# A planner that orders a fused attention and gated product: two projections in flight, a different choice of banks, choices redrawn every 8 phases, and separate buffers in the tail

## The chip, the cores and the metric

The kernel runs on one core of a Trainium2 chip. Times are microseconds of that core. The time before is 669.75 us, the median of three runs (669.70 to 669.76). In the tables TensorE is PE (its weight loads are PEld), ScalarE is ACT, VectorE is DVE, GpSimd is POOL, and SyncE, which issues most transfers, is SP.

## The reference

The inputs are bfloat16, 2048 rows of 512 elements. With `xn` the layer-normalised input, the output is `x + s * g`:

```python
xn = _layernorm(x)                                   # 2048 x 512
q  = (xn @ wq) in 32 heads of 16;  k = xn @ wk;  v = xn @ wv   # one k and one v for all heads
p  = softmax(q k^T / sqrt(16))                       # 32 heads x 2048 x 2048
s  = (p v, heads side by side) @ wo                  # 2048 x 512
g  = silu(silu(xn @ w1) @ w2)                        # 512 -> 1792 -> 512
return x + s * g
```

The exponentials of 32 x 2048 x 2048 scores are most of the work.

## The kernel before

**No order is written by hand.** Python code in the kernel simulates the five engines with fixed durations (the class `Planner`) while the program is being made, and the order in which it places operations is the order of each engine's program. On the chip every engine runs its list in order, with semaphore waits. So the planner's choices are fixed in the program; nothing is decided at run time.

**The score tiles.** The scores are cut into 2048 tiles of 128 keys x 512 queries of one head. A tile's matmul uses only 32 rows of the TensorE array, so up to four tiles of different row groups run side by side. One such bundle is called a phase (`do_S`, L1001 on). Each tile fills one of seven PSUM banks (0 to 6); the eighth, `OB`, collects the attention output. A bank comes free when its exponential has been taken, in one of two ways:

- An A tile: ScalarE's Exp (L1717), for up to three banks in one instruction if they are equally spaced neighbours. The result goes to `pa_sb`, which has 26 slots; the number of slots in use is `a_pressure()`.
- A D tile: VectorE turns the score into the bit pattern of an approximate power (L1002) in `db_sb`. Three more shifted copies of it are made by GpSimd (L1202) in `ds_sb`, four tiles at a time.

**The products after it.** An A tile takes part in one matmul with V (L1282), a D tile in four. These matmuls have 32 columns, and four of different column groups run side by side; such a bundle of four is called a round here. Rounds of the attention product (`do_pv`) and rounds of the projections (L511) have the same shape. A change between a phase (32 rows x 128 columns) and rounds (128 x 32) is a change of the array's mode; the planner counts `SWITCH` 105 ns for it.

**The projections.** A job is one projection tile: 56 of kind `h` (w1, 4 rounds each), 16 `z` (w2, 14 rounds), 15 `q` (4 rounds) and 12 `w` (wo, 4 rounds) besides those of the start and the tail. A job takes a bank of the seven when it starts (`start_jobs`), runs its rounds between phases, and gives the bank back when the instruction that evacuates it has been placed: for `h` and `z` a tanh on ScalarE (L669) and then a product on VectorE (L671). Jobs start in the order of their pace (a share of the tiles assigned). `can_start` allows one such job at a time (two in the prologue), counted until the bank comes back, and none while `a_pressure()` is above `START_Z` 4 or `START_H` 8. Since a phase holds at most four tiles and leaves rows idle when it holds three, a `z` job can also run a quarter of one of its rounds in a phase's idle row group; these are called pieces (L618).

**A step of TensorE.** `pe_step` looks whether a phase is possible (`s_phase_ready`: at least three banks free, and not later than ScalarE needs it; a fourth bank is waited for only up to `STOL4` 0 ns past that), and otherwise places a round: of the attention if `a_pressure()` has reached a limit, else of a job, else of the attention. `do_S` decides how many tiles of the phase are D tiles: with four banks free `N4` 2 (`J4` 2 while a job is active), with three `N3` or `J3` 1, less if VectorE's backlog is long. Limits pass through `vary`, which multiplies them with a random factor within `SPREAD`. The random numbers come from a list of ten seeds, each used for `STRETCH` 64 phases.

**The tail.** The last four output tiles (r = 0 to 3) have no further scores beside them. Their product with wo ends in banks; r = 0 and 2 (`EVR`) are evacuated by ScalarE into `xn_sb` (L714) and multiplied by VectorE (L716), r = 1 and 3 are evacuated and multiplied by VectorE at once (L719). For r < 3 the result and the residual `xr_sb` are summed by TensorE with an identity matrix (L1503) and copied to `ob_sb` by ScalarE (L1508); for r = 3 VectorE adds (L731). The results lie in `fin_sb`, whose two halves alternate. The four stores are issued by SP (L725).

Of the kernel before, what the change touches and what calls it, by code (L numbers as in the profile page):

```python
# [46 lines left out]
MM = 216.0  # L47
BLG = 0
NEAR, AHEAD = 18, 0.6
SWITCH, SKEW = 105.0, 10.0  # L50
# [245 lines left out]
def bass_recurrent_scan__grouped_kv_mqa__dense_activation_silu__prompt_kernel(  # L296
# [30 lines left out]
    with ExitStack() as es:  # L327
# [56 lines left out]
        def vary(x):  # L384
            return x * (1.0 + SPREAD * (rng[-1].random() - 0.5)) if rng else x
        outs = []
        PH.clear()
# [112 lines left out]
        def job(kind, arg, pace, rounds, consume, preds=(), bk=None, mode="C", gate=None):  # L500
            jb = Job()
            jb.kind, jb.arg, jb.pace, jb.rounds, jb.consume = kind, arg, pace, rounds, consume
            jb.preds, jb.bank, jb.fixed, jb.mode, jb.gate = preds, bk, bk is not None, mode, gate
            jb.due, jb.pos, jb.end, jb.got, jb.left, jb.piece, jb.prev = None, 0, len(rounds), set(), len(rounds), None, None
            jb.tasks = {}
            jobs.append(jb)
            return jb
# [187 lines left out]
        def mk_z(tt, pace):  # L695
            c, r = divmod(tt, 4)

            def consume(jb, op):
# [10 lines left out]
                    lambda k, rows: w2_sb[rows, k, :], lambda k: ["w2", ("u", k)])  # L709

        def scaled(tt, b, r=None):
            k = tt % 2
            if r in EVR:
                ev = pl.add(Task(AC, 490.0, lambda a: a.activation(xn_sb[:, r, :], bank(b), ACT.Copy, scale=0.25),  # L714
                                 [("ps", b)], [("xn", r)], 0))
                fin_task[tt] = Task(DV, 333.0, lambda v: v.tensor_tensor(fin_sb[:, k, :], xn_sb[:, r, :], tmp_sb[:, tt % 8, :], ALU.mult),  # L716
                                    [("xn", r), ("tmp", tt % 8)], [("fin", k)], SC_PRIO, [ev, tmp_task[tt], fin_task.get(tt - 2)], ports=2)
                return fin_task[tt]
            fin_task[tt] = Task(DV, T_P, lambda v: v.scalar_tensor_tensor(  # L719
                out=fin_sb[:, k, :], in0=bank(b), scalar=0.25, in1=tmp_sb[:, tt % 8, :], op0=ALU.mult, op1=ALU.mult),  # L720
                [("ps", b), ("tmp", tt % 8)], [("fin", k)], 0 if r is None else SC_PRIO, [tmp_task[tt], fin_task.get(tt - 2)])
            return fin_task[tt]
# [4 lines left out]

        def final(tt, b):
            k = tt % 2
            t1 = scaled(tt, b)  # L730
            t2 = Task(DV, 333.0, lambda v: v.tensor_tensor(ob_sb[:, tt % 4, :], fin_sb[:, k, :], xr_sb[:, tt % 4, :], ALU.add),  # L731
                      [("fin", k), ("xr", tt % 4)], [("ob", tt % 4)], -1, [t1, xr_task[tt], out_task.get(tt - 4)], ports=2)
            fin_task[tt], out_task[tt] = t2, store(tt, t2)
            return t1, t2
# [54 lines left out]
        for tt in range(NT - 4):  # L789
            specs.append((2 * NOC * (tt // 4 + 1) + 1.2 + 0.5 * (tt % 4), 2, ("w", tt)))  # L790
        specs.sort()
        for pace, _, sp in specs:
# [140 lines left out]
        def s_phase_ready():  # L933
# [20 lines left out]
            n = min(n, 4)  # L954
            while n > NMIN and bt[n - 1][0] > need + STOL4:
                n -= 1
# [3 lines left out]
            if n < 4:  # L960
                r = max(r, need - EARLY)
            return r
# [43 lines left out]
        def do_S(t):  # L1006
# [8 lines left out]
            if n <= 1:  # L1015
                want = 1 if ab > 2 * a_low else 0
            elif n == 2:
                want = 1 if ab > a_low else 0
            else:
                queue = sum(len(q) for g in range(st["gO"], min(st["gO"] + 2, NG)) for q in pvq[g])  # L1020
                held = any(not a.fixed for a in active)
                if held:
                    want = J4 + (queue < vary(Q4)) if n == 4 else J3 + (queue < vary(Q3))
                else:
                    want = N4 if n == 4 else max(N3, 2 * (queue < vary(QUEUE)))
                if ab > a_low:
                    want = 2
            pj = None
            late = [b for r, b in bank_times()[n:] if r <= t + LATE]
            if bl > one or not want_d():  # L1030
# [28 lines left out]
            banks = sorted(banks[:len(sl) + nd])  # L1059
            best = None  # L1060
            for c in combos(banks, len(sl)):
                key = (len(c) > 1 and len(set(y - x for x, y in zip(c, c[1:]))) > 1, c[-1] - c[0])
                if best is None or key < best[0]:
                    best = (key, c)
            abanks = best[1]
            solo = False
            if SOLO and len(sl) == 3:
# [70 lines left out]
            if dslots:  # L1138
                make_shifts()
            return True  # L1140

# [185 lines left out]
        def make_norm(g):  # L1327
# [6 lines left out]
            if g == NG - 1:  # L1334
# [9 lines left out]
                rcp_sb[:, k, :].unsqueeze(2).to_broadcast([P, NQ // 32, DH]), ALU.mult),  # L1344
                [("F", k), ("rcp", k)], [("otr", oi % 2, e)], -1, [t2, t2_task.get(oi - 2)], ports=2))
            norm[("m", g)] = t3
# [27 lines left out]
        def can_start(jb, pro):  # L1374
            near = not pro and closing()
            if jb.pace > progress() + (AHEAD if near else 1e-9):
# [5 lines left out]
            if not pro and not near and a_pressure() > (START_Z if jb.kind == "z" else START_H):  # L1382
# [48 lines left out]
        def finish(jb, op):  # L1431
            if jb.left == 0:
                tasks = jb.consume(jb, op)
                last = tasks[-1]

                def fin(op, jb=jb):
# [16 lines left out]
        def make_tail():  # L1453
# [20 lines left out]
        def tail_round(t):  # L1474
# [11 lines left out]
            for n, (r, part) in enumerate(tail["sums"]):  # L1486
# [3 lines left out]
                if part == 0 and (xr_task.get(tt) is None or xr_task[tt].op is None or len(tail["items"]) > 3):  # L1490
                    continue
                rr = pl.ready(PE, [("fin", tt % 2)] if part else [("xr", tt % 4)], () if part else [("ps", tb[4 + r])]) if tb[4 + r] in pool_free else INF
                if rr <= t + 20:
# [4 lines left out]
        def do_tail(t, it):  # L1498
            if it[0] == "s":
                r, part = tail["sums"].pop(it[1])  # L1500
                tt = 4 * (NC - 1) + r
                src = fin_sb[:, tt % 2, :] if part else xr_sb[:, tt % 4, :]
                pl.place(PE, MM, lambda pe: pe.matmul(bank(tb[4 + r]), lhsT=ident[:, :], rhs=src, start=part == 0, stop=part == 1),  # L1503
                         [("fin", tt % 2) if part else ("xr", tt % 4)] + [("id", i) for i in range(4)], [("ps", tb[4 + r])],
                         t0=max(t, pe_start(pl.clk[PE], "F")))
# [54 lines left out]
        def pe_step():  # L1560
# [11 lines left out]
            lim = vary(PRESS if jr[0] != "go" else PRESS_Z if jr[1].kind == "z" else PRESS_H)  # L1572
            if pr and pr[0] == "go" and (a_pressure() >= lim or closing()):
                col = ("pv", pr[1])
# [106 lines left out]
        def act_step():  # L1681
# [10 lines left out]
            if q:  # L1692
                q = [u for u in q if u.vis <= max(t, q[0].vis) + 25]
                while len(q) > 1 and (len(set(y.bank - x.bank for x, y in zip(q, q[1:]))) > 1 or abs(q[1].bank - q[0].bank) != 1):
                    q.pop()
                if q[0].solo:
                    q = q[:1]
                elif len(q) > 1 and any(u.solo for u in q):
                    q = q[:[u.solo for u in q].index(True)]
                n = len(q)  # L1700
                while n:
# [118 lines left out]
```

## Time and profile before

| what | value |
|---|---|
| median of three runs | 669.75 us (669.70 to 669.76) |
| span of the profiled execution, first to last instruction | 667.9 us |
| PE, ACT, DVE, POOL busy | 657.8, 652.8, 613.6, 561.9 us |
| TensorE clock granted | 1.000 |
| score tiles: taken by ScalarE, by VectorE | 1312, 736 |
| matmuls (all kinds) | 8972 |

The page gives the profiled execution's span, and no other time of its own; the median of the runs stands 1.85 us above that span. A row of the list of groups reads: line, engine, operation, output and inputs, shape, number; then busy time in us and mean ns of one; then the engine's idle time before it and what ended it. Busy times are unions, and instructions of ScalarE, VectorE and TensorE overlap their neighbours, so the mean of one instruction is longer than the distance from its start to the next one's start. Where the text below counts phases, rounds or distances, they are counted over the trace's rows in order of time.

### The profile page before, as it was taken

Reading aid. Unit: us, or ns where it says so; the run is one execution under the profiler, and the core shown is the slowest. Engines: PE = TensorE matmul, PEld = TensorE weight load, DVE = VectorE, ACT = ScalarE, POOL = GpSimd, SP = SyncE. Lnnn points to the kernel's source line nnn. Section 1 sums busy time; section 2 is a strip of 40 time slices with the busy share of each in tenths; the row PEclk is TensorE's granted clock in tenths of the full one; section 3 lists DMA queues with packets and bytes.
Section 4 is the critical chain, followed back from the end, with each engine's and each line's share of the span. In section 5 each row is a group of like instructions: output and inputs, shape, how many; then the busy total and the mean of one; then the engine's idle time right before and its main releaser. Section 6 shows DMA issues by size and latency. Waiting matters only on the chain.

```text
span 667.9 us, 21230 instructions
## 1 busy us (share of the span) xinstructions
PE 657.8 (98%) x8972; PEld 190.3 (28%) x8973; DVE 613.6 (92%) x1093; ACT 652.8 (98%) x767; POOL 561.9 (84%) x560
## 2 busy tenths in 40 slices
PE   8999999999999999999999999999999999999997
PEld 4322222222222222222222222222222322222222
DVE  8989999999899999989999899999999999998995
ACT  6999999999999999999999999999999999999997
POOL 3059889999898889998989888999899989897972
PEclk9999999999999999999999999999999999999999
DMA  9500000000000000000000010000000000000000
GB/s 302 164 9 2 3 1 2 2 3 2 1 2 18 19 18 18 1 2 2 2 2 2 18 32 18 2 2 2 2 2 2 2 18 18 17 18 2 2 2 33
DMA packets 11501, 12.86 MB, mean 19 GB/s; under 512 B 1808, under 2 KB 10768, under 8 KB 11408
## 3 DMA queue, kind: packets, MB, share of 16 engines
q1 hardware_dynamic: 10928, 10.78, 5.0%
q8 instruction: 72, 1.18, 0.7%
q0 software_dynamic: 192, 0.46, 0.2%
q10 hardware_dynamic: 288, 0.26, 0.1%
q14 instruction: 21, 0.17, 0.1%
HBM read 8.95 MB, written 2.10 MB: 17 GB/s over the span
## 4 chain that ended last, share of the span: by engine, by line
PE 88%; ACT 6%; DVE 4%; issue 1%; DMA 0%; ACTq 0%; DVEq 0%
PE ps L1282 38%; PE ps L866 29%; PE ps L511 20%; ACT pa_sb L1717 6%; DVE db_sb L1002 1%; DVE stats_sb L458 1%; ACT t_sb L669 1%; DMA ds_sb<-in_A_x_dram 0%; DVE fin_sb L719 0%; PE ps L527 0%; DVE xnT_sb L538 0%; DVE xn_sb L487 0%; DVE ob_sb L731 0%; DVE mv_sb L462 0%; DVE on_sb L1316 0%
## 5 line engine op out<-in xcount | busy, mean ns | idle before, releaser
L1717 ACT ACTIVATE pa_sb<-ps 128x1024 bf16<-128x1024 f32 (+2 forms) x670 | 617.0, 1027 | 4.8 <-PE ps L866 3.5
L1202 POOL INT64_ADD ds_sb<-db_sb x544 | 554.0, 1040 | 64.2 <-DVE otr_sb L1342 31.7
L1002 DVE TENSOR_SCALAR db_sb<-ps 128x512 uint16<-128x512 f32 x736 | 475.4, 683 | 40.0 <-PE ps L866 28.6
L1282 PE MATMUL ps<-ds_sb,v_sb 128*32 128x512 bf16 x2208 | 268.7, 383 | 0.0
L866 PE MATMUL ps<-qt_sb,kt_sb 32*128 32x512 bf16 x2048 | 251.2, 384 | 3.9 <-ACT pa_sb L1717 0.9
L1282 PE MATMUL ps<-pa_sb,v_sb 128*32 128x512 bf16 x1316 | 240.9, 382 | 0.0
L1282 PE MATMUL ps<-db_sb,v_sb 128*32 128x512 bf16 x736 | 169.3, 383 | 0.0
L866 PEld LDWEIGHTS ps<-qt_sb,kt_sb 32*128 32x128 bf16 x2048 | 62.8, 91 | 276.7 <-ACT pa_sb L1717 151.2
L1282 PEld LDWEIGHTS ps<-ds_sb,v_sb 128*32 128x32 bf16 x2208 | 65.6, 95 | 62.3 <-issue 44.6
L511 PE MATMUL ps<-xnT_sb,w_sb 128*32 128x512 bf16 x896 | 71.7, 383 | 0.0
L1282 PEld LDWEIGHTS ps<-pa_sb,v_sb 128*32 128x32 bf16 x1316 | 58.8, 95 | 37.9 <-issue 24.7
L511 PE MATMUL ps<-w_sb,u_sb 128*32 128x512 bf16 x820 | 64.1, 383 | 0.0
L1282 PEld LDWEIGHTS ps<-db_sb,v_sb 128*32 128x32 bf16 x736 | 42.2, 95 | 20.2 <-issue 14.7
L669 ACT ACTIVATE t_sb<-ps 128x512 bf16<-128x512 f32 x72 | 44.9, 623 | 0.0
L671 DVE SCALAR_TENSOR_TENSOR u_sb<-t_sb,ps 128x512 bf16<-128x512 bf16 x56 | 38.2, 683 | 1.0
L618 PE MATMUL ps<-w_sb,u_sb 32*128 32x512 bf16 x76 | 29.2, 384 | 0.0
L511 PEld LDWEIGHTS ps<-xnT_sb,w_sb 128*32 128x32 bf16 x896 | 17.1, 94 | 26.1 <-issue 21.1
L1359 POOL DMA_DIRECT2D kt_sb<-kt_sb x4 | 2.3, 566 | 23.9 <-DVE var_sb L481 8.1
L1338 DVE STREAM_TRANSPOSE f_sb<-ps 128x512 f32<-128x512 f32 x31 | 21.9, 706 | 0.0
L511 PEld LDWEIGHTS ps<-w_sb,u_sb 128*32 128x32 bf16 x820 | 15.2, 95 | 22.5 <-issue 19.3
L511 PE MATMUL ps<-wo_sb,on_sb 128*32 128x512 bf16 x256 | 18.9, 383 | 0.0
L511 PE MATMUL ps<-xnT_sb,wq_sb 128*32 128x512 bf16 x240 | 18.7, 384 | 0.1
(74 smaller groups left out, 180.8 us busy)
## 6 DMA issues: line engine op xcount, KB each, us to landing
w_sb<-in_B_w_dram SPq DMA_DIRECT2D x2, 1792.0 KB, 13.4
xr_sb<-in_A_x_dram SPq DMA_DIRECT2D x16, 128.0 KB, 2.6
out_dram<-ob_sb SPq DMA_DIRECT2D x16, 128.0 KB, 1.7
ds_sb<-in_A_x_dram SPq DMA_DIRECT2D x3, 512.0 KB, 6.6
wq_sb<-in_A_wq_dram SPq DMA_DIRECT2D x1, 512.0 KB, 4.9
wo_sb<-in_A_wo_dram SPq DMA_DIRECT2D x1, 512.0 KB, 16.2
kt_sb<-kt_sb POOLq DMA_DIRECT2D x4, 112.0 KB, 3.7
ds_sb<-in_A_x_dram ACTq DMA_DIRECT2D x2, 128.0 KB, 2.9
```

The costliest lines, as they stand in the source:

```text
L458: ts_ = pl.add(Task(DV, 593.0, lambda v, t=t: v.bn_stats(stats_sb[:, t, :], x_tile(t)), [xkey(t)], [("st", t)], 1 + j, gate=(lambda j=j: S ...
L511: last = h.matmul(bank(b)[32 * j:32 * (j + 1), 0:n], lhsT=lhs(j), rhs=rhs, start=start, stop=stop, tile_position=(0, 32 * j), skip_group_c ...
L618: return (lambda pe: pe.matmul(bank(b), lhsT=lhs(k, rows, 0, P), rhs=rhs(k, rows), start=False, stop=last, tile_position=(32 * i, 0), skip ...
L669: t1 = Task(AC, 490.0, lambda a: a.activation(t_sb[:, k, :], src, ACT.Tanh, scale=scale), [held], [("t", k)], 0, [t0])
L671: t2 = Task(DV, T_P, lambda v: v.scalar_tensor_tensor(out=dst, in0=t_sb[:, k, :], scalar=1.0, in1=src, op0=ALU.add, op1=ALU.mult), [held, ...
L866: return pe.matmul(bank(b), lhsT=kt_sb[32 * i:32 * i + 32, g % 2, kt * P:(kt + 1) * P], rhs=qt_sb[32 * i:32 * i + 32, (g // 2) % NQR, :], ...
L1002: bt.P[i] = pl.add(Task(DV, T_P, lambda v: v.tensor_scalar(db_sb[:, bt.b, i * NQ:(i + 1) * NQ], bank(b), 128.0 * LOG2E, 128.0 * (SHIFT_BET ...
L1202: whole["po"].append(pl.add(Task(PO, T_P64, lambda g, cols=cols: g.int64_add(ds_sb[:, s, cols].bitcast(U64), db_sb[:, bt.b, cols].bitcast( ...
L1282: h = pe.matmul(bank(OB)[32 * i:32 * (i + 1), cols], lhsT=lhs, rhs=rhs, start=s0, stop=s1, tile_position=(0, 32 * i), skip_group_check=True)
L1338: t1 = pl.add(Task(DV, T_TR, lambda v: v.transpose(f_sb[:, k, :], bank(OB)), [("ps", OB)], [("F", k)], 1, [norm.get(("m", g - 2))]))
L1359: kt1[c] = pl.add(Task(PO, T_SWDGE, lambda e: e.dma_start(kt_sb[DH:P, 1, cols], kt_sb[0:P - DH, 0, cols]), [("kt0", k) for k in range(4 * ...
L1717: op = pl.place(AC, 0.8333 * NQ * n + T_AF, lambda a: a.activation(pa_sb[:, s * NQ:(s + n) * NQ].rearrange("p (b n) -> p b n", n=NQ), ps3[ ...
```

## The change

- `TWO = 1`: `can_start` counts only jobs that still have rounds to run against the limit, so a second job may start while the first one's bank waits for its evacuation. In all no more than two jobs outside the prologue hold a bank.
- `JPICK = 1`, `JTOL`: a starting job no longer takes the bank that comes free first, but among those free within 30 ns of it the one that leaves most neighbouring pairs among the other banks.
- `START_H` goes from 8 to 11.
- The seeds are 84 instead of 10, `STRETCH` is 8 instead of 64, `SPREAD` 0.4 instead of 0.3. After each phase `redraw` sets further choices at random: with a chance of 3% the number of D tiles of the next phase, with 3% that ScalarE's instruction takes one bank instead of a pair, with 10% whether a round of the attention or of a job goes first, with 10% that a D tile may join a phase up to 200 ns late, with 5% that a phase may wait up to 250 ns for a fourth bank, with 5% that a phase of fewer banks may start up to 400 ns sooner, and with 20% each which banks the A tiles and a starting job take.
- Tail: r = 0 and 2 use the halves of `fin_sb`, r = 1 and 3 their own tile of `xn_sb`; `EVR` is (1, 3), and only r = 0 and 1 (`SUMS = 2`) are summed by TensorE; r = 2 and 3 are added by VectorE.
- `CHAIN`, `BUNCH`, `APICK`, `PR_OTR`, `PR_OB` and `FAR` are new names whose values leave the code as it was.

```diff
-SEEDS, STRETCH, SPREAD = (4812, 312, 1660, 4615, 1697, 8414, 4190, 8770, 5102, 5729), 64, 0.3
+SEEDS = (
+    3820, 2220, 5745, 350, 5151, 6989, 5911, 6177, 6265, 4479, 5498, 6172, 361, 2787, 4955, 618,
...
+STRETCH, SPREAD = 8, 0.4
...
+TWO = 1
+JPICK, JTOL, APICK = 1, 30.0, 0
+R_WANT, R_SPLIT, R_FIRST, R_LATE, R_TOL, R_BANK = 0.03, 0.03, 0.1, 0.1, 0.05, 0.2
...
-START_Z, START_H = 4, 8
+START_Z, START_H = 4, 11
...
-RH, EVR, SC_PRIO, MT_EARLY = 6, (0, 2), 0, 1
+RH, EVR, SC_PRIO, MT_EARLY = 6, (1, 3), 0, 1
...
+        def redraw():
+            if not rng:
+                return
+            r = rng[-1]
+            pick.update(want=r.choice((0, 1, 2)) if r.random() < R_WANT else None, split=r.random() < R_SPLIT,
+                        first=r.choice(("pv", "job")) if r.random() < R_FIRST else None,
+                        late=r.random() * 200.0 if r.random() < R_LATE else 0.0,
+                        tol=r.random() * 250.0 if r.random() < R_TOL else 0.0,
+                        early=r.random() * 400.0 if r.random() < R_TOL else 0.0,
+                        abank=r.random() if r.random() < R_BANK else None, jbank=r.random() if r.random() < R_BANK else None)
...
+        def fin_of(tt, r=None):
+            if r is None or r % 2 == 0:
+                k = tt % 2 if r is None else r // 2
+                return fin_sb[:, k, :], ("fin", k)
+            return xn_sb[:, r, :], ("xn", r)
...
-            while n > NMIN and bt[n - 1][0] > need + STOL4:
+            while n > NMIN and bt[n - 1][0] > need + pick["tol"]:
...
+            if pick["want"] is not None:
+                want = min(pick["want"], n - 1)
...
-                if len([a for a in active if not a.fixed]) >= lim or not pool_free:
+                if len([a for a in active if not a.fixed and (a.left or not TWO)]) >= lim or not pool_free:
+                    return False
+                if TWO and not pro and len([a for a in active if not a.fixed]) >= 2:
                     return False
...
-                    jb.bank = min((r, b) for r, b in bank_times())[1]
+                    bt = bank_times()
+                    if JPICK:
+                        ok = [b for r, b in bt if r <= max(t, bt[0][0]) + JTOL]
+                        gone = [u.bank for u in units[st["expn"]:]]
+                        jb.bank = min(ok, key=lambda b: bank_key(b, pro_free(b), ok))
...
-            tail["sums"] = [(r, part) for part in range(2) for r in range(3)]
+            tail["sums"] = [(r, part) for part in range(2) for r in range(SUMS)]
...
-                if r < 3:
+                if r < SUMS:
                     stt[r] = pl.add(scaled(tt, tb[r], r))
                 else:
-                    for tk in final(tt, tb[r]):
+                    for tk in final(tt, tb[r], r):
                         pl.add(tk)
```

More of the change, by code (lines that the diff above doesn't have):

```diff
@@ L48 @@
 BLG = 0
+TWO = 1
+BUNCH = 0
+SUMS = 2
+FAR = 1
+JPICK, JTOL, APICK = 1, 30.0, 0
+PR_OTR, PR_OB = -1, -1
+CHAIN, AHEAD_T, START_T = '', 0.3, 11
+R_WANT, R_SPLIT, R_FIRST, R_LATE, R_TOL, R_BANK = 0.03, 0.03, 0.1, 0.1, 0.05, 0.2
 NEAR, AHEAD = 18, 0.6
@@ L385, in vary @@
             return x * (1.0 + SPREAD * (rng[-1].random() - 0.5)) if rng else x
+        pick = dict(want=None, split=False, first=None, late=0.0, tol=0.0, early=0.0, abank=None, jbank=None)
+        def redraw():
[8 more added lines that the diff above has]
+                        abank=r.random() if r.random() < R_BANK else None, jbank=r.random() if r.random() < R_BANK else None)
         outs = []
@@ L726, in store, with final @@
                                [("ob", tt % 4)], [("out", tt)], 0, [t2], dma=128 * 1024, on_place=outs.append))
[L728 to L732, printed above, removed]
+        def final(tt, b, r=None):
+            t1 = scaled(tt, b, r)
+            src, key = fin_of(tt, r)
+            t2 = Task(DV, 333.0, lambda v: v.tensor_tensor(ob_sb[:, tt % 4, :], src, xr_sb[:, tt % 4, :], ALU.add),
+                      [key, ("xr", tt % 4)], [("ob", tt % 4)], PR_OB if r is None else 1,
+                      [t1, xr_task[tt], out_task.get(tt - 4)], ports=2)
             fin_task[tt], out_task[tt] = t2, store(tt, t2)
@@ L791, in bass_recurrent_scan__grouped_kv_mqa__dense_activation_silu__prompt_kernel @@
         specs.sort()
+        if BUNCH:
+            specs = [(BUNCH * int(p / BUNCH) if sp[0] != "q" else p, k, sp) for p, k, sp in specs]
         for pace, _, sp in specs:
@@ L1027, in do_S @@
                     want = 2
+            if pick["want"] is not None:
+                want = min(pick["want"], n - 1)
             pj = None
-            late = [b for r, b in bank_times()[n:] if r <= t + LATE]
+            late = [b for r, b in bank_times()[n:] if r <= t + pick["late"]]
             if bl > one or not want_d():
@@ L1059, in do_S @@
             banks = sorted(banks[:len(sl) + nd])
-            best = None
+            best, like = None, []
             for c in combos(banks, len(sl)):
                 key = (len(c) > 1 and len(set(y - x for x, y in zip(c, c[1:]))) > 1, c[-1] - c[0])
+                if APICK:
+                    key = (key[0], key[1] > len(c) - 1, pairs_of([x for x in pro_free(-1) if x not in c]) * -1, key[1])
                 if best is None or key < best[0]:
                     best = (key, c)
+                if len(set(y - x for x, y in zip((c[0] - 1,) + c, c))) == 1:
+                    like.append(c)
             abanks = best[1]
+            if like and pick["abank"] is not None:
+                abanks = like[int(pick["abank"] * len(like))]
             solo = False
@@ L1375, in can_start @@
             near = not pro and closing()
-            if jb.pace > progress() + (AHEAD if near else 1e-9):
+            chain = CHAIN and not pro and jb.kind in CHAIN and any(
+                not a.fixed and a.left == 0 and a.kind in "hz" and (a.ev is None or a.ev.op is None or a.ev.op.end > pl.clk[PE]) for a in active)
+            if jb.pace > progress() + (AHEAD if near else AHEAD_T if chain else 1e-9):
                 return False
@@ L1381, in can_start @@
                 return False
-            if not pro and not near and a_pressure() > (START_Z if jb.kind == "z" else START_H):
+            if not pro and not near and a_pressure() > (START_T if chain else START_Z if jb.kind == "z" else START_H):
                 return False
@@ L1385, in can_start, with pro_free, pairs_of, bank_key @@
                 lim = 2 if pro else 1
-                if len([a for a in active if not a.fixed]) >= lim or not pool_free:
-                    return False
-            return True
+                if len([a for a in active if not a.fixed and (a.left or not TWO)]) >= lim or not pool_free:
+                    return False
+                if TWO and not pro and len([a for a in active if not a.fixed]) >= 2:
+                    return False
+            return True
+        def pro_free(b):
+            held = {a.bank for a in active if not a.fixed} | set(fixed) | {b}
+            return [x for x in BANKS if x not in held]
+        def pairs_of(rest):
+            pairs, k = 0, 0
+            while k < len(rest) - 1:
+                if rest[k + 1] == rest[k] + 1:
+                    pairs += 1
+                    k += 2
+                else:
+                    k += 1
+            return pairs
+        def bank_key(b, rest, ok):
+            if JPICK == 3:
+                return (-pairs_of(rest), -pairs_of(sorted(x for x in ok if x != b)), b)
+            if JPICK == 4:
+                return (-pairs_of(sorted(x for x in ok if x != b)), -pairs_of(rest), b)
+            return (-pairs_of(rest), -b if JPICK == 2 else b)
         def start_jobs(t):
@@ L1400, in start_jobs @@
                 if not jb.fixed:
-                    jb.bank = min((r, b) for r, b in bank_times())[1]
+                    bt = bank_times()
[3 more added lines that the diff above has]
+                        jb.bank = min(ok, key=lambda b: bank_key(b, pro_free(b), ok))
+                        if pick["jbank"] is not None:
+                            jb.bank = ok[int(pick["jbank"] * len(ok))]
+                    else:
+                        jb.bank = bt[0][1]
                     pool_free.remove(jb.bank)
@@ L1501, in do_tail @@
                 tt = 4 * (NC - 1) + r
-                src = fin_sb[:, tt % 2, :] if part else xr_sb[:, tt % 4, :]
+                src, key = fin_of(tt, r) if part else (xr_sb[:, tt % 4, :], ("xr", tt % 4))
                 pl.place(PE, MM, lambda pe: pe.matmul(bank(tb[4 + r]), lhsT=ident[:, :], rhs=src, start=part == 0, stop=part == 1),
-                         [("fin", tt % 2) if part else ("xr", tt % 4)] + [("id", i) for i in range(4)], [("ps", tb[4 + r])],
+                         [key] + [("id", i) for i in range(4)], [("ps", tb[4 + r])],
                          t0=max(t, pe_start(pl.clk[PE], "F")))
@@ L1572, in pe_step @@
             lim = vary(PRESS if jr[0] != "go" else PRESS_Z if jr[1].kind == "z" else PRESS_H)
-            if pr and pr[0] == "go" and (a_pressure() >= lim or closing()):
+            if pr and pr[0] == "go" and (a_pressure() >= lim or closing() or pick["first"] == "pv") and pick["first"] != "job":
                 col = ("pv", pr[1])
@@ L1693, in act_step @@
                 q = [u for u in q if u.vis <= max(t, q[0].vis) + 25]
-                while len(q) > 1 and (len(set(y.bank - x.bank for x, y in zip(q, q[1:]))) > 1 or abs(q[1].bank - q[0].bank) != 1):
+                while len(q) > 1 and (len(set(y.bank - x.bank for x, y in zip(q, q[1:]))) > 1 or abs(q[1].bank - q[0].bank) > FAR):
                     q.pop()
@@ L1699, in act_step @@
                     q = q[:[u.solo for u in q].index(True)]
+                if len(q) > 1 and pick["split"]:
+                    q = q[:1]
                 n = len(q)
```

21 lines of the change are left out of this document (12 added, 9 removed), and 5 rows, old and new, of the table SEEDS.

## The prediction

> **What bounds the kernel now.** I read the totals first, then the table of 40 slices, the groups by shape, and then the timeline of TensorE.
>
> ```profile
> PE 657.8 (98%) x8972; PEld 190.3 (28%) x8973; DVE 613.6 (92%) x1093; ACT 652.8 (98%) x767; POOL 561.9 (84%) x560
> ...
> PEclk9999999999999999999999999999999999999999
> ```
>
> Two engines show 98%, so the totals don't name the bound. Overlaps have to be taken off.
>
> ```profile
> L1717 ACT ACTIVATE pa_sb<-ps 128x1024 bf16<-128x1024 f32 x622 | 588.5, 1048 | 4.1 <-PE ps L866 2.9
> L669 ACT ACTIVATE t_sb<-ps 128x512 bf16<-128x512 f32 x72 | 44.9, 623 | 0.0
> L1717 ACT ACTIVATE pa_sb<-ps 128x512 bf16<-128x512 f32 x40 | 22.8, 623 | 0.7 <-PE ps L866 0.6
> L1717 ACT ACTIVATE pa_sb<-ps 128x1536 bf16<-128x1536 f32 x8 | 11.5, 1477 | 0.0
> ```
>
> A ScalarE pair lasts 1048 ns, but its median distance to the next start is 905 ns; a single or a tanh takes 478, a triple 1331. So ScalarE needs 622 x 905 + (40 + 72) x 478 + 8 x 1331 = 627 us. The first score matmul is at 10.9 us and the last half exponentials end at 660.1, 649 us apart: some 20 us of true slack, which the busy total hides because neighbours overlap. VectorE has 54 us idle.
>
> ```profile
> 407.78 0.39 PE L866 MATMUL ps<-qt_sb,kt_sb 32*128 32x512 bf16 x3
> 408.10 0.62 PE L511 MATMUL ps<-wo_sb,on_sb 128*32 128x512 bf16 x8
> 408.65 0.39 PE L866 MATMUL ps<-qt_sb,kt_sb 32*128 32x512 bf16 x3
> 408.97 0.40 PE L511 MATMUL ps<-wo_sb,on_sb 128*32 128x512 bf16 x4
> ```
>
> This is TensorE's beat: from a phase to its rounds 0.32 us, from two rounds (8 matmuls) to the next phase 0.55 us. Over 20 to 657 us there are 634 phases. Phases take 321 ns (3 matmuls) or 325 (4); a run of 2, 3, 4 rounds takes 548, 764, 980, that is 216 a round and 116 for the way back. So a phase costs 321 + 116 = 437 ns whatever it holds, and a round 216 ns. 634 x 437 + 1608 x 216 + 4.3 (other modes) = 628.7 of 637 us; the other 8.4 us are waits before phases, 5.6 of them after 50 us. TensorE is the bound, and only fewer phases, fewer rounds or shorter waits help.
>
> The whole program has 641 phases for 2048 tiles, 3.195 each: 516 with three, 125 with four. Turning four phases of three into three of four saves one phase, so each additional phase of four saves 437 / 3 = 146 ns.
>
> **The change part by part.**
>
> *Two projections.* Following each job's matmuls to its evacuation, a job holds a bank for 391 us of the span; 236 us of it run rounds, 160 us wait for the evacuation (1.9 us for an `h` or `z`, 0.9 for a `q` or `w`). Of 98 hand-overs 44 follow the last evacuation within 300 ns: there the next job was waiting for the bank. At most these 44 x 1.5 us = 66 us are overlapped, and as much becomes free of jobs. From 60 to 657 us 35% of the phases without a job hold four tiles (88 of 249), 9% of those with one (33 of 350). 66 us are some 66 phases: 26% of them, 17, become phases of four, 17 x 146 ns = 2.5 us. The other end: while two banks are held, five are left, and each such phase might hold a tile less: 66 / 3.2 = 20 more phases, +9.0 us. The nearest row, 35% against 9%, prices a held bank at a quarter of a tile per phase, not a whole one; I take -1.2, half of the gain. The jobs' rounds are the same in number, and no instruction or transfer is added.
>
> *Bank of a job.* Forty single exponentials are at most 20 broken pairs, 2 x 478 - 905 = 51 ns each: 1.0 us of ScalarE, under its 20 us of slack: 0. Were that slack gone, it would be worth 1.0. START_H 11 lets an `h` start with up to three more slots filled; rounds only change places: 0, bounded by the hand-overs above.
>
> *The draws.* What can choices be worth? I cut the body into nine stretches of 64 phases and took the matmuls of the scores (first fence, one row of three) and the projections (second) in each.
>
> ```profile
> 339.32:406.00 66.68, 25.07 (x200) 6.25 (x202) 1.00 0.05 14
> 406.00:466.97 60.97, 25.08 (x207) 6.27 (x208) 1.00 0.02 6
> ...
> sum 572.11, PE 225.71 PEld 56.37; mean PE 25.08 PEld 6.26
> ```
>
> ```profile
> 339.32:406.00 66.68, 21.74 (x272) 5.13 (x272) 1.00 0.05 14
> 406.00:466.97 60.97, 13.82 (x176) 3.00 (x176) 1.00 0.02 6
> ```
>
> The columns are the window, its length, and PE's busy time with the matmuls in brackets. The length less 54 ns for each projection matmul, by the scores: (66.68 - 14.69) / 200 = 0.2600 us a tile in the first, (60.97 - 9.50) / 207 = 0.2486 in the second. Over all nine the mean is (572.11 - 104.11) / 1849 = 0.2531, the best three average 0.2492. If every stretch ran like those: 1849 x 0.0039 = 7.2 us. At the other end the draws are disturbances: 5% of 641 phases waiting 125 ns is 4.0 us of TensorE, with the rounds queued behind each wait, and 3% split pairs is 19 x 51 ns, under ScalarE's slack. So -7.2 to +4.0. I take -4.3, six tenths of the gain, as the good stretches are a row of this trace and choices by 8 phases can combine good pieces; most phases draw nothing that costs, since a fourth bank is often there. VectorE's 54 us would carry it: a D tile more is 607 ns of it from start to start.
>
> *Tail.* From the timeline of the last microseconds:
>
> ```profile
> 662.65 0.40 DVE L716 TENSOR_TENSOR fin_sb<-xn_sb,tmp_sb 128x512 bf16<-128x512 bf16 x1
> ...
> 663.08 0.69 DVE L719 SCALAR_TENSOR_TENSOR fin_sb<-ps,tmp_sb 128x512 bf16<-128x512 f32 x1
> ...
> 663.60 1.74 ACT L1508 ACTIVATE ob_sb<-ps 128x512 bf16<-128x512 f32 x3
> ...
> 664.02 0.42 DVE L731 TENSOR_TENSOR ob_sb<-fin_sb,xr_sb 128x512 bf16<-128x512 bf16 x1
> ```
>
> The third copy of ScalarE ends at 665.34 and releases the last store. It goes: two copies end at 664.76. VectorE gets a second add (0.34 from start to start): from 662.15 two evacuations (0.60), two products (0.34) and two adds (0.34) end at 664.7. SP then issues the same four stores. Gain 0.5; between 0, if the products on ScalarE's evacuation of r = 3 come late, and 0.6.
>
> *Prologue.* More than two jobs may hold banks there. TensorE's idle stretches at 12.87 and 20.31 us (0.65 and 0.60) end with an exponential and a normalisation, not a job's bank: 0, bounds -1 and +1.
>
> Sum: -1.2 - 4.3 - 0.5 = -6.0; against the profiled execution 667.9 gives 661.9 of span, and with the 1.85 us around it **663.7 us**.
>
> **The rivals.** The median of 669.75 is the base of each.
>
> *More than that.* All 2.5, 7.2 and 0.6, and half of the 5.6 us of waits: -13.1, 656.6. For it: ScalarE's 20 us and VectorE's 54 are not used up. Against: no stretch of the trace comes near all of these at once.
>
> *Hidden anyway.* TensorE is never idle, so other choices only permute rounds, and the count of phases stays at 641: the tail's 0.5 alone, 669.2. Against: the spread over stretches.
>
> *The second bank is missed (slower).* Each two-held phase loses a tile: +9.0 with the draws at nothing and the tail's -0.5: 678. It decides against the change from 40 lost tiles on (12 phases, 5.5 us, the other terms). For it: no phase starts under three banks while ScalarE has work. Against: a job already costs only 0.26 phases of four per phase.
>
> *The draws only disturb:* +4.0, less the tail: 673.
>
> *The clock.* It is 1.000 in every window, with waits before phases of up to 0.54 us (at 29 us). Waits of 250 ns are shorter. If 1% of the span ran at half clock, it would cost 6.7 us: 676 with the rest at nothing and the tail's gain. The Trainium skill (TensorE: Matmul & The Clock Gate, "A second HAM failure mode: psum-queue depth-cycling") reports a kernel whose micro-idles while cycling through PSUM banks made the clock fall and recover again and again; by that rule added waits for a bank could bring this about, and the trace, which cycles through seven banks with waits and full clock, doesn't bear it out.
>
> **How the numbers follow.** Forecast, 660 to 668.3: 0.64. More, below 660: 0.21. Hidden: 0.05. Second bank: 0.05. Disturbance: 0.04. Clock: 0.01. About 0.2% (1.3 us, 668.4 to 671.1) is what can be told from no change. Faster 0.85, same 0.05, slower 0.10. Range 656.5 to 669.5: from the largest gain, which leaves out the little below it, to the hidden case; the slower ones, 0.10, lie outside.
>
> **What would show it.** Fewer than 641 phases, about 620 to 630, with more than 125 of four tiles; a single phase still at 437 ns and a round at 216. Hand-overs where a job's rounds begin before the last evacuation ends. About 650 ScalarE exponentials at unchanged lengths. Two L1508 copies and two adds in the tail, ending near 0.5 us sooner after the last transpose. The prediction is wrong if the phases stay at 641 or rise, if waits before phases grow past 8.4 us, or if ScalarE's idle time shows it as the new bound.

## The result: 4.2 us faster, and the profile after

The changed kernel takes 665.53 us (665.46 to 665.61) against 669.70 us, a ratio of 0.9937 (95% interval 0.9926 to 0.9948). The forecast was 663.7. Its profiled execution has a span of 663.7 us, 4.2 us less than before.

The totals and the clock of the page after, then its groups of exponentials, D tiles and quarter rounds (lines have moved: phases are L904, attention rounds L1329, projection rounds L540, quarter rounds L647, exponentials L1800):

```profile
PE 652.6 (98%) x8958; PEld 188.4 (28%) x8959; DVE 614.8 (93%) x1097; ACT 650.6 (98%) x783; POOL 565.7 (85%) x564
...
PEclk9999999999999999999999999999999999999999
```

```profile
L1800 ACT ACTIVATE pa_sb<-ps 128x1024 bf16<-128x1024 f32 x593 | 562.2, 1048 | 1.3 <-PE ps L904 0.6 <-PE ps L647 0.2
L1040 DVE TENSOR_SCALAR db_sb<-ps 128x512 uint16<-128x512 f32 x740 | 476.7, 682 | 35.4 <-PE ps L904 20.6 <-PE ps L647 8.4 <-POOL ds_sb L1249 1.0
...
L1800 ACT ACTIVATE pa_sb<-ps 128x512 bf16<-128x512 f32 x85 | 48.1, 622 | 1.0 <-PE ps L904 0.8
L647 PE MATMUL ps<-w_sb,u_sb 32*128 32x512 bf16 x120 | 46.1, 385 | 0.0
L698 ACT ACTIVATE t_sb<-ps 128x512 bf16<-128x512 f32 x72 | 44.9, 624 | 0.0
L1800 ACT ACTIVATE pa_sb<-ps 128x1536 bf16<-128x1536 f32 x11 | 16.0, 1485 | 0.0
```

The quarter rounds (L647) are the news. Before, 76 quarter rounds of `z` ran in idle row groups of phases, as this line of the profile before shows; now it is 120.

```profile
L618 PE MATMUL ps<-w_sb,u_sb 32*128 32x512 bf16 x76 | 29.2, 384 | 0.0
```

The exponentials that take a single bank went from 40 to 85, the opposite of what the bank choice seemed to be for.

TensorE's beat is unchanged. A phase of three matmuls takes 321 ns until its rounds, of four 325; two rounds and the way back 548, three 764, four 980. This is its timeline at one place after:

```profile
400.42 0.39 PE L904 MATMUL ps<-qt_sb,kt_sb 32*128 32x512 bf16 x3
400.74 0.62 PE L540 MATMUL ps<-xnT_sb,w_sb 128*32 128x512 bf16 x8
401.29 0.39 PE L904 MATMUL ps<-qt_sb,kt_sb 32*128 32x512 bf16 x3
```

The 4.2 us can be accounted for by the lengths of phases and rounds, with the numbers counted over the two traces:

| | before | after | worth |
|---|---|---|---|
| phases (437 ns) | 641 | 638 | -1.3 us |
| quarter rounds, each in place of 54 ns of a round | 76 | 120 | -2.4 us |
| D tiles (three more matmuls, 162 ns) | 736 | 740 | +0.6 us |
| waits before phases, from 20 us on | 8.4 us | 7.4 us | -1.0 us |
| sum | | | -4.1 us |
| last attention round ends, to the end of the span | 7.44 us | 7.47 us | 0 |

The account closes against the body's part to some tenths of a microsecond: the last attention round ends at 656.19 instead of 660.43 us. The tail gave nothing. The last attention round before, then after:

```profile
660.14 0.29 PE L1282 MATMUL ps<-pa_sb,v_sb 128*32 128x256 bf16 x4
```

```profile
655.90 0.29 PE L1329 MATMUL ps<-pa_sb,v_sb 128*32 128x256 bf16 x4
```

The account is not finer than about half a microsecond. Before, TensorE also ran six bundles of matmuls with zeros at 24 to 26 us (0.65 us), which the planner places when it has nothing else for TensorE; after, there are none from 20 us on. How far the row of waits holds them is not settled.

### The profile page after: what moved, and what is told of

The parts are those of the page before. It is cut to its first block, busy times and chain, and to the rows that moved or that the text cites. A ratio compares the mean times of both kernels' runs of the same rounds, so it can differ in the third digit from the quotient of the medians.

```text
span 663.7 us, 21210 instructions
## 1 busy us (share of the span) xinstructions
PE 652.6 (98%) x8958; PEld 188.4 (28%) x8959; DVE 614.8 (93%) x1097; ACT 650.6 (98%) x783; POOL 565.7 (85%) x564
## 4 chain that ended last, share of the span: by engine, by line
PE 90%; ACT 4%; DVE 4%; DMA 0%; issue 0%; ACTq 0%; DVEq 0%
PE ps L1329 40%; PE ps L904 30%; PE ps L540 19%; ACT pa_sb L1800 4%; DVE db_sb L1040 1%; DVE stats_sb L487 1%; PE ps L556 1%; DMA ds_sb<-in_A_x_dram 0%; ACT t_sb L698 0%; DVE xn_sb L516 0%; DVE xnT_sb L567 0%; DVE ds_sb L1243 0%; DVE fin_sb L754 0%; DVE f_sb L1385 0%; DVE var_sb L512 0%
## 5 line engine op out<-in xcount | busy, mean ns | idle before, releaser
L1800 ACT ACTIVATE pa_sb<-ps 128x1024 bf16<-128x1024 f32 (+2 forms) x689 | 615.1, 1002 | 2.3 <-PE ps L904 1.3
L1329 PE MATMUL ps<-ds_sb,v_sb 128*32 128x512 bf16 x2220 | 265.1, 383 | 0.2 <-DVE ds_sb L1243 0.2
L904 PE MATMUL ps<-qt_sb,kt_sb 32*128 32x512 bf16 x2048 | 250.0, 384 | 3.8 <-ACT pa_sb L1800 1.5
L1329 PE MATMUL ps<-pa_sb,v_sb 128*32 128x512 bf16 x1312 | 231.5, 383 | 0.0
L1329 PE MATMUL ps<-db_sb,v_sb 128*32 128x512 bf16 x740 | 161.5, 383 | 0.0
L904 PEld LDWEIGHTS ps<-qt_sb,kt_sb 32*128 32x128 bf16 x2048 | 62.4, 90 | 275.2 <-ACT pa_sb L1800 150.6
L1329 PEld LDWEIGHTS ps<-ds_sb,v_sb 128*32 128x32 bf16 x2220 | 63.5, 95 | 62.2 <-issue 45.5
L540 PE MATMUL ps<-xnT_sb,w_sb 128*32 128x512 bf16 x896 | 71.1, 383 | 0.0
L1329 PEld LDWEIGHTS ps<-pa_sb,v_sb 128*32 128x32 bf16 x1312 | 56.7, 95 | 43.1 <-issue 31.0
L540 PE MATMUL ps<-w_sb,u_sb 128*32 128x512 bf16 x776 | 62.4, 383 | 0.0
L647 PE MATMUL ps<-w_sb,u_sb 32*128 32x512 bf16 x120 | 46.1, 385 | 0.0
L1329 PEld LDWEIGHTS ps<-db_sb,v_sb 128*32 128x32 bf16 x740 | 39.8, 95 | 20.3 <-issue 15.4
L540 PEld LDWEIGHTS ps<-xnT_sb,w_sb 128*32 128x32 bf16 x896 | 18.2, 95 | 24.1 <-issue 16.1
L540 PEld LDWEIGHTS ps<-w_sb,u_sb 128*32 128x32 bf16 x776 | 15.3, 95 | 20.0 <-issue 17.0
L540 PE MATMUL ps<-wo_sb,on_sb 128*32 128x512 bf16 x256 | 19.3, 382 | 0.0
L540 PE MATMUL ps<-xnT_sb,wq_sb 128*32 128x512 bf16 x240 | 18.7, 383 | 0.0
```

The lines of the kernel that those rows point to most:

```text
L540: last = h.matmul(bank(b)[32 * j:32 * (j + 1), 0:n], lhsT=lhs(j), rhs=rhs, start=start, stop=stop, tile_position=(0, 32 * j), skip_group_c ...
L647: return (lambda pe: pe.matmul(bank(b), lhsT=lhs(k, rows, 0, P), rhs=rhs(k, rows), start=False, stop=last, tile_position=(32 * i, 0), skip ...
L904: return pe.matmul(bank(b), lhsT=kt_sb[32 * i:32 * i + 32, g % 2, kt * P:(kt + 1) * P], rhs=qt_sb[32 * i:32 * i + 32, (g // 2) % NQR, :], ...
L1329: h = pe.matmul(bank(OB)[32 * i:32 * (i + 1), cols], lhsT=lhs, rhs=rhs, start=s0, stop=s1, tile_position=(0, 32 * i), skip_group_check=True)
L1800: op = pl.place(AC, 0.8333 * NQ * n + T_AF, lambda a: a.activation(pa_sb[:, s * NQ:(s + n) * NQ].rearrange("p (b n) -> p b n", n=NQ), ps3[ ...
```

## The experiments

In all but the last of them the order of every engine's program comes out of the planner anew, so one edited line changes thousands of places. Twelve kernels ran. Their times stand beside the kernel before on the same chip (669.7 to 669.9).

**Draws off, in both kernels.** The lists are emptied; limits keep their values, nothing is redrawn.

```diff
-SEEDS, STRETCH, SPREAD = (4812, 312, 1660, 4615, 1697, 8414, 4190, 8770, 5102, 5729), 64, 0.3
+SEEDS, STRETCH, SPREAD = (), 64, 0.3
```

> The kernel before with an empty list of seeds, so every limit keeps its plain value. Theory 1 (the sum of the prediction: draws are most of the gain, the second projection little): the ten old seeds of 64 phases are a coarse choice and worth less than half of what the new list is worth, so this is 671 to 672. Theory 2 (the new list of draws is worth no more than the old one, and the gain of 4.2 us is that of the two projections and of the choice of banks): the old list is worth as much as the new one, 4 to 6 us, so this is 674 to 676.

> The changed kernel with an empty list of seeds: no limits varied, no choices redrawn. Theory 1: it loses the 4.3 us of the draws and lies at 670, 1 to 2 us under the old kernel without draws. Theory 2: it lies 4 to 6 us under the old kernel without draws, and 4 to 6 above the changed kernel with its list, at 670 to 671. What tells them apart is the distance to the old kernel without draws: 1.7 or about 5.

Measured: the old kernel 673.83 us (ratio to before 1.0062, 1.0047 to 1.0077), the new one 669.83 (1.0008, 0.9998 to 1.0017). Both lists are worth about the same, 4.1 and 4.3 us, and the distance without draws is 4.0. That looked like theory 2: the second projection and the bank choice make the whole difference. The trace showed at least what the old order lacks. The last `z` job isn't done when the scores are; its rounds (w_sb, u_sb) and its evacuation stand in the tail, ahead of the last product with wo. Timeline of the old kernel without draws (L511 projection rounds, L669 and L671 the evacuation, L714 the tail's):

```profile
661.27 1.89 PE L511 MATMUL ps<-w_sb,u_sb 128*32 128x512 bf16 x30
...
662.85 3.77 PE L511 MATMUL ps<-wo_sb,on_sb 128*32 128x512 bf16 x64
663.21 0.60 ACT L669 ACTIVATE t_sb<-ps 128x512 bf16<-128x512 f32 x1 [3.24 <-PE ps L511]
663.84 0.69 DVE L671 SCALAR_TENSOR_TENSOR tmp_sb<-t_sb,ps 128x512 bf16<-128x512 bf16 x1 [0.69 <-ACT t_sb L669]
666.01 1.09 ACT L714 ACTIVATE xn_sb<-ps 128x512 bf16<-128x512 f32 x2 [2.21 <-PE ps L511]
```

From the end of the last attention round to the end of the span it takes 10.6 us, against 7.4 in the kernel before.

**One projection at a time, without draws.**

```diff
-TWO = 1
+TWO = 0
```

> The changed kernel without draws and with TWO = 0: a job starts only when the last one's bank is back. Theory 1: overlap is worth 1.2 us, so it is 1.2 above the changed kernel without draws. Theory 2: the overlap is worth 3 to 5 us, because hand-overs with a waiting job delay the z rounds that could fill idle row groups and make phases of three wait. If the second bank does harm (rival of 678), it is faster than the changed kernel without draws.

Measured 673.23 us (1.0052, 1.0036 to 1.0069): 3.4 above the changed kernel without draws.

**First free bank, without draws.**

```diff
-JPICK, JTOL, APICK = 1, 30.0, 0
+JPICK, JTOL, APICK = 0, 30.0, 0
```

> The changed kernel without draws and with JPICK = 0: a starting job takes the bank that comes free first, as before; TWO stays 1. The prediction's term for the bank was 0 (51 ns for each broken pair, under ScalarE's slack): then this lies within 0.5 us of the changed kernel without draws, 669.8. Theory 2b (overlap pays only where the two held banks leave neighbours for ScalarE's pairs): it loses about as much as without the overlap, 3 to 4 us, 673 to 674, and more ScalarE exponentials take one bank than the 33 of the changed kernel without draws.

Measured 674.53 us (1.0069, 1.0055 to 1.0083), 4.7 above. The reason given for it fell: single-bank exponentials (halves of the tail left out) are 30, not more than the 31 with the bank choice. Each part seems to be worth nothing without the other, which is odd. The traces show where each order spends more than the changed kernel without draws: with one projection at a time, five more phases (644 against 639) and 1.1 us more after the last attention round; with the first free bank, 20 fewer quarter rounds (76 against 96) and longer waits, less three phases. Why the planner's orders differ so, they don't show. That raised the question whether single orders can be compared at all.

**Another pace, in both kernels.** `J_END` moves the pace of the projections slightly. It is as harmless an edit as the planner offers.

```diff
-J_BASE, J_END, MIXJ = 0.1, 1.0, 2
+J_BASE, J_END, MIXJ = 0.1, 1.5, 2      # and 2.0
```

> The kernel before without draws, with J_END 1.5 instead of 1.0: the projections' pace ends half a group of heads earlier, so that each job may start up to 1.6% sooner. No theory so far gives this edit a price of its own. Theory 2 (the second projection and the bank choice are worth 4 us by what they do): this is about 673.8 as with 1.0, and 4 us above its new counterpart. Theory 3 (any small edit makes another order, and orders scatter by about 2 us, so the 4 us between two single orders may be luck): it is anywhere from 670 to 676, and the distance to its new counterpart is not 4 us, of either sign.

> The changed kernel without draws, with J_END 1.5. Theory 2: about 669.8 as with 1.0, 4 us under the old one with the same pace. Theory 3: it scatters by about 2 us, 668 to 675.

> The kernel before without draws, with J_END 2.0. Theory 2: about 673.8, less at most the 3 us that the z job left over in the tail costs it at 1.0 if the earlier pace lets that job end before. Theory 3: 670 to 676, and not 4 us above its new counterpart.

> The changed kernel without draws, with J_END 2.0. Theory 2: about 669.8. Theory 3: 668 to 675; over the three paces the mean of old less new is nearer to 0 than to 4.

| without draws, us | J_END 1.0 | 1.5 | 2.0 | mean |
|---|---|---|---|---|
| old kernel | 673.83 | 673.39 | 671.60 | 672.9 |
| changed kernel | 669.83 | 674.71 | 673.05 | 672.5 |
| old less changed | 4.0 | -1.3 | -1.4 | 0.4 |

Theory 2 falls as it was put, with 4 us at every pace. The 4.0 us was one order against one other. Both times that the same edit is made on both sides the sign turns, and single orders scatter by some 1 to 2.5 us. The mean, 0.4 us, is not told from 0 by three pairs (their differences scatter by 3.1, so the mean is uncertain by about 1.8). The changed kernel's medians lie between two groups of executions, which the last section describes; with the lower group of each, the difference is 0.9. By the same measure the 3.4 and 4.7 us of the two experiments above aren't shown to belong to their edits; whether the second projection or the bank choice alone is worth a microsecond stays open.

One thing is common to all orders with two projections that ran: from the end of the last attention round to the end of the span they take 7.2 to 7.5 us. The four orders without draws that allow one projection take 8.0 to 11.0. Over the three paces the changed kernel's end is 2.4 us shorter on average, so 1.5 to 2 us are lost again in its body. In the kernel before, its list of draws had an order without the left-over (7.4), so nothing of it was to be had there.

**Other seeds.** 84 numbers taken at random in place of the list.

> The changed kernel with 84 other seeds, not chosen for anything. By its program it has 628 phases instead of 638, 165 of them with four tiles. If fewer phases are what makes the time (the main lever of the prediction), it must be 10 x 0.437 = 4 us faster than the changed kernel, 661. If disturbances of the draws cost more than phases give (the rival of 673), it is slower than the changed kernel without draws, 673 to 683, and TensorE's waits before phases must be above the 7.4 us of the changed kernel, or its rounds more.

Measured 681.99 us (1.0184, 1.0169 to 1.0199), the slowest of all, with the fewest phases: 628 counted in its trace, 165 with four tiles. Without any draws the changed kernel took 669.8 to 674.7 us in its three paces: this list costs 7 to 12 us.

```profile
span 680.1 us, 21358 instructions
...
PE 663.1 (97%) x9042; PEld 195.4 (29%) x9042; DVE 618.5 (91%) x1107; ACT 654.0 (96%) x799; POOL 569.0 (84%) x568
```

PE is busy 663.1 of 680.1 us, 17.0 us idle; after, 652.6 of 663.7, 11.1. Against the changed kernel: phases -10 x 0.437 = -4.4 us; quarter rounds 84 instead of 120, +1.9; D tiles 748 instead of 740, +1.3; waits before phases 19.9 instead of 7.4 us, +12.5. Sum +11.3 of 16.4 us. Two losses stand in no term. From 20 us to the last phase 39 rounds hold fewer than four matmuls, instead of 5; such a round takes as long as a full one (two rounds of five matmuls with the way back 538 ns, of eight 548), so some 2.8 us more go unused. And 17 bundles of matmuls with zeros run there instead of none, 1.7 us. They make up most of the remaining 5.1 us, though the waits as counted may hold a part of them. Fewer phases are no gain if they are bought with waits, D tiles and rounds that are not full.

**Other seeds, nothing redrawn.**

```diff
-R_WANT, R_SPLIT, R_FIRST, R_LATE, R_TOL, R_BANK = 0.03, 0.03, 0.1, 0.1, 0.05, 0.2
+R_WANT, R_SPLIT, R_FIRST, R_LATE, R_TOL, R_BANK = 0, 0, 0, 0, 0, 0
```

> The 84 other seeds again (682.0 with them), but with all the chances of the redraw at 0, so that only the limits vary, by up to 20%. If the redrawn choices are what disturbs, the waits before phases fall from 19.9 us to 10 to 13 and the time to 674 to 677; if the varied limits disturb as much, it stays above 680.

Measured 676.42 us (1.0097, 1.0082 to 1.0113), waits 14.6 us. Without the redrawn choices this list costs 5.6 us less; the waits lie just above the 10 to 13 expected. This is again one order against one other: the limits and the redrawn choices take their numbers from the same list in turn, so the edit also changes the limits.

**No quarter rounds, without draws.** All 14 rounds of a `z` run as rounds.

```diff
-PIECE_MIN = {"z": 4, "h": 9, "q": 9, "w": 9}
+PIECE_MIN = {"z": 99, "h": 9, "q": 9, "w": 9}
```

> The changed kernel without draws, with no quarter rounds of z in idle row groups (96 of them without this edit). If a quarter round saves 54 ns of TensorE, a quarter of a round, it is 5.2 us slower, 675; if the saved rounds are given back as waits, it is within 1 us of 669.8.

Measured 677.95 us (1.0121, 1.0107 to 1.0135), 8.1 above the changed kernel without draws, where 5.2 was expected for the rounds alone. The groups of `z` matmuls, of the changed kernel without draws and then of this one:

```profile
L533 PE MATMUL ps<-w_sb,u_sb 128*32 128x512 bf16 x800 | 65.0, 383 | 0.0
L640 PE MATMUL ps<-w_sb,u_sb 32*128 32x512 bf16 x96 | 36.9, 385 | 0.0
```

```profile
L533 PE MATMUL ps<-w_sb,u_sb 128*32 128x512 bf16 x896 | 73.0, 383 | 0.0
```

96 matmuls move back into rounds: 24 rounds, 5.2 us. Besides, there are three phases more (1.3 us) and 1.7 us more waits, less four D tiles (0.6). The sum is 7.6; of the two groups of times told of at the end, the faster ones are 7.7 apart. So the account at 54 ns for a quarter round closes here too. The time alone doesn't prove the 54 ns, since single orders scatter by 1 to 2.5 us.

**A store on ScalarE's queue.** The changed kernel, with the store of r = 1 issued by ScalarE.

```diff
-                    out_task[tt] = store(tt, t2)
+                    out_task[tt] = store(tt, t2, AC if r else SP)
```

> The changed kernel; of its last four stores the one of r = 1 is issued by ScalarE, which has just copied that tile, instead of by SP. In the changed kernel SP issues the four one after another, 659.99 to 661.81 us, and the last result is ready at 660.67. If this queue sets the end, the last issue ends 0.45 to 0.5 us sooner: 665.0 to 665.1. If the last result or the landing sets it, 665.5.

The order of all four engines' instructions is the same as in the changed kernel, so this is the one experiment free of the scatter of orders. Measured 665.44 us (0.9933, 0.9920 to 0.9945), 0.09 under the changed kernel, which the two intervals don't tell apart; against the kernel before on the same chip it is 4.42 us faster, the changed kernel 4.17. The issues, of the changed kernel and then with two queues:

```profile
659.37 1.30 ACT L1589 ACTIVATE ob_sb<-ps 128x512 bf16<-128x512 f32 x2
...
659.99 1.81 SPq L760 DMA_DIRECT2D out_dram<-ob_sb  x4
660.18 0.42 DVE L766 TENSOR_TENSOR ob_sb<-xn_sb,xr_sb 128x512 bf16<-128x512 bf16 x1
```

```profile
660.09 1.32 SPq L760 DMA_DIRECT2D out_dram<-ob_sb  x3
660.28 0.42 DVE L766 TENSOR_TENSOR ob_sb<-xn_sb,xr_sb 128x512 bf16<-128x512 bf16 x1
660.80 0.35 ACTq L760 DMA_DIRECT2D out_dram<-ob_sb  x1
```

Measured from the end of the last attention round, the last issue ends at 5.12 us instead of 5.62: the 0.5 us expected. SP's wait for the last landing ends at 6.75 instead of 7.03, so about half is left. Behind the queue the landings themselves come one after another: with two queues the four landings are 0.34 to 0.52 us apart. It is the fastest kernel that ran, by no more than the measurement's uncertainty.

## Why the prediction was right, and for which reasons it was not

The time lies in the range, the sign was forecast, and 4.2 us against 6.0 is a fair size. The steps did worse than the sum, and that the sum came near is in part luck: more than half of the gain came from a row that the sum left out.

*What bounds the kernel* held. TensorE's phases, rounds and waits account for 4.1 of the 4.2 us, at the lengths read from the trace before.

*"Only fewer phases, fewer rounds or shorter waits help"* held, but the step after it failed: I priced only fewer phases. 620 to 630 were expected, 638 came, 1.3 us. The larger part, 2.4 us, came from rounds moved into idle row groups. The quarter rounds were described ahead of the prediction, 440 phases had an idle row group, and no term of the sum was about them. The 628 phases of the other seeds, 16 us slower, show that their number was the wrong measure of an order.

*Two projections, -1.2.* Jobs held banks at the same time for 27 us in all (sum of holds 424, union 397; some 5 us before), not 66, and the time without a job did not grow (the union was 391 before). The step from overlap to free time failed: held time only moved and lengthened, a `z` running 7.6 us on average instead of 6.3 while phases went between its rounds. What the edit is worth isn't settled; without draws it went with a tail free of left-over rounds. `START_H` 11 was not tried alone, so its 0 stays open.

*Bank of a job, 0.* Singles doubled where 20 broken pairs were to be mended (without draws the changed kernel has 31, so the rise came with the draws), at no visible cost: ScalarE's distances remain 905 and 478 ns, and 593 x 905 + (85 + 72) x 478 + 11 x 1331 = 626 us is what it needs, 627 before. Its slack held, so the term of 0 stands in the final order.

*The draws, -4.3.* Averaged over three paces the changed kernel without draws takes 672.5 us, so the list is worth 7.0; the old list, from 672.9, 3.2. The difference of 3.8 agrees with the term, within an uncertainty of nearly 2 us. The mechanism I gave for it did not hold. The time per tile in nine stretches, net of projections, fell only from 0.2541 to 0.2536 us (counted alike in both traces); the gain by this measure is 0.9 us, and the projection rounds left out of it got fewer. And the row I took the draws' other end from, +4.0, was far too mild: an unchosen list cost 7 to 12 us over no draws. That draws pay only when chosen was the real condition, and the program's text could not tell that these are.

*Tail, -0.5.* The compute ended sooner as worked out: from the start of the last transpose of `on_sb` to the last result 3.20 us instead of 3.63. It was worth nothing. The term missed SP: its four issues take 1.81 us one after another and begin with the first result, which came no sooner, 3.80 us after the last attention round against 3.79. I had counted the stores as "the same four" and not asked when their queue runs out. The trace before shows it already:

```profile
664.22 1.80 SPq L725 DMA_DIRECT2D out_dram<-ob_sb  x4
```

The four issues follow each other within 0.05 us until 666.02, so the third copy, which ended at 665.34, did not release the last store as I had read it; the last issue waited for the one before it.

*The clock, 0.01.* It stayed at 1.000 in the changed kernel. In other orders it did fall, at a cost of 1.1 to 1.4 us and not the 6.7 that I priced; see below.

## What to carry to other kernels

When a planner writes the order, one order against one other says little: a harmless edit moved these kernels by 0.4 to 4.9 us, as much as the change itself, so a part has to be tried over several orders before it is given a price. Count what an order costs the bounding engine (phases, rounds, waits, and the work fitted into idle row groups) rather than one of these. At the end of a kernel, follow the queue that issues the stores before pricing the work ahead of it.

## What the hardware did that I had not expected

In three of the kernels without draws the profile shows TensorE's clock at half for 3.41 us, once, from a point between 31 and 40 us on, and in the executions of these and of two more the times fall into two groups whose means lie 1.1 to 1.4 us apart (new kernel without draws: 669.7 to 670.0 and 671.0 to 671.3). The three profiled executions with the drop belong to the slower group, the two without it to the faster. Windows of TensorE, columns window, length, busy time with matmuls, clock, DMA share, GB/s; first the changed kernel, then the same without draws:

```profile
30.00:35.00 5.00, 4.98 (x81) 1.00 0.02 5
35.00:40.00 5.00, 4.42 (x72) 1.00 0.07 23
40.00:45.00 5.00, 4.72 (x64) 1.00 0.00 0
```

```profile
30.00:35.00 5.00, 4.72 (x74) 1.00 0.00 1
35.00:40.00 5.00, 3.84 (x57) 0.89 0.09 28
40.00:45.00 5.00, 5.00 (x56) 0.76 0.00 0
```

Ahead of the drop TensorE was busy 1.84 of 3.00 us (36 to 39 us), with its longest single pause 0.65 us. With J_END 1.5 it was busy for the same 1.84 us there and the profiled execution kept the full clock, so these pauses alone don't decide it, and that they are the cause isn't shown. The Trainium skill (TensorE: Matmul & The Clock Gate, "A second HAM failure mode: psum-queue depth-cycling") describes a kernel that cycles through PSUM banks with short pauses of TensorE, at which the clock falls and recovers again and again. These runs agree in part: here it fell once, and the pause of 0.65 us waited for `kt_sb`, not for a bank. Half the clock for 3.41 us is at most 1.7 us of work, and the groups differ by 1.1 to 1.4. The profiled execution of the new kernel without draws belongs to the slower group, so its span of 669.2 us is not the 669.83 less the usual 1.85.
